# Loading the second half batch's q and k by head halves in 768-byte runs, in a rearranged opening

## The chip, the cores and the metric

The kernel runs on one core of a Trainium2 chip. The metric is device time in microseconds (us) of one execution. Engines are named as in the profile: PE is TensorE (its matmuls; PEld its weight loads), DVE is VectorE, ACT is ScalarE, POOL is GpSimd, SP is SyncE.

## The reference

Attention over q, k, v of shape (4 batches, 8 heads, 768 tokens, 64), each query seeing the first 8 keys and its last 96, with a slope times distance as bias; then a feed-forward layer on the 3072 x 512 result.

```python
scores = scale * np.matmul(q, k.transpose(0, 1, 3, 2))
keep = is_global | is_local            # pos < 8, or 0 <= rel < 96
scores = np.where(keep, scores - slopes[:, None, None] * dist, -1e9)
a = softmax(scores); attn = np.matmul(a, v)
x = attn.transpose(0, 2, 1, 3).reshape(B * S, H * D)
h = np.maximum(x @ w_in, 0.0)          # w_in 512 x 2048
out = (h * h @ w_out)                  # w_out 2048 x 512
```

## The kernel before, in words

The work goes by eight half batches of 384 tokens, three tiles of 128 tokens each: x0 and x1 are the halves of the first batch. For a tile, tokens lie on the partitions as loaded; PE transposes q and k so that the head dimension lies on the partitions (names `trp`), DVE or ACT copies the result from PSUM ("evacuates" it) to `q` and `k`. A query tile meets two key tiles: its own ("o") and the one before with the global keys in its first 32 columns ("b", kept in `kb`; its values in `vb`). Scores `sp` go through an exponential on ACT; attention `av`, its normalisation (a reciprocal `rec` and a product `tm` on DVE), a transpose (`trx`) and a copy give `xt`, the input of layer 1 (`hps`, L717), whose weights `w_in_sb` come in four quarters c0 to c3. Layer 2 is `yps`. Later half batches take other paths, which the change does not touch; large parts of their layers use sums of weights and of activations in place of products.

The opening, some 20 us, is the first batch's attention up to layer 1. It is written as jobs in the string `OPENING`: T0 and T1 transpose tiles 0 and 1 of q and k together; Q2 to Q5 and K2 to K5 one tile each; P are matmuls that put the bias into PSUM (tiles 0 to 2), S scores, A attention, X the transposes to `xt`, V the copies to `vb`. F and G are layer 1 of x0 (F of its first tile, G of the other two). So F0, G00 and G01 read c0; F1, G10 and G11 read c1; A50 and A51 are the attention of tile 5, which needs the values of tile 5 (v5).

Every operation on every engine, every load too, stands in one table, `ORDER`, written out as text ("p" PE, "a" ACT, "d" DVE, "s" SP, "l" a load on POOL, with numbers in the order of listing; behind the dot the PSUM banks). Each engine runs its operations strictly in that order. `LOADING` only gives the loads their numbers. Costs such as {"ACT": 0.51, "DVE": 0.36} stand beside operations and do nothing when the program runs.

The loads: SP and ACT issue four loads for tiles 0 and 1 (f32, then cast by `first_tiles`). All others are issued on POOL, which converts to f16 on the way: one tile of 128 tokens and 8 heads is 1024 runs of 256 bytes in memory (`rows`, L396), written as 128 bytes each; a quarter of `w_in` is 512 runs of 2 KB (L454). x1's q and k are staged in memory that `w_mix` uses later, so they are called w_mix in the profile. Loads on POOL take eight semaphores in turn, so that the ninth waits until the first has landed.

The copies are all one helper, L256 on ACT and L258 on DVE.

Of the kernel before, what the change touches and what calls it, by code (L numbers as in the profile page):

```python
# [9 lines left out]
FP16 = mybir.dt.float16  # L10
# [3 lines left out]
P = 128  # L14
# [5 lines left out]
OPENING = """T0 P1b T1 K3 P0o S0o S1b Q2 K2 P1o S1o P2o P2b A00 S2o A01 S2b Q5 Q3 A11 X01 Q4 V1 S3o A10  # L20
K4 X11 A20 X00 K5 X10 A21 S4o S4b S3b X21 X20 F1 G11 V2 S5o V3 S5b G10 F0 A40 V4 A30 G01 A41
# [4 lines left out]
LOADING = """v1 k3 k2 q2 v0 q3 q4 q5 k5 v2 k4 c1 v3 c0 v4 v5 c3 c2"""  # L26
# [30 lines left out]
a73 p29.6 d68 p18.5 d72 p28.4 a74 p26.3 l19 p36.1 d54 a69 p35.2 p30.7 a86 d70 p33.54 d85 a71 d91
p39.16 a67 p40.27 a77 d63 p37.3 a82 d75 l17 a78 d62 p41.5 a92 d79 d76 p38.0 d84 d80 p45.4 d83
l21 a97 p48.1 d96 a101 l20 a98 p44.2 a89 p47.5 d107 l23 p46.7 a112 p42.0 d111 a108 d110 a93
p43.2 d109 p53.1 a87 p52.5 d102 p50.4 p49.7 a113 l22 d120 d100 a90 d105 p59.6 l27 a116 d119 a103  # L60
d106 p55.3 p51.1 l29 d94 a122 a88 d128 p65.2 l28 a104 d95 a117 p64.4 a118 p58.5 a129 a136 d114
p60.0 d99 a137 l30 d146 d191 p54.3 l24 p62.6 d115 d205 l25 p57.1 a133 p56.4 d125 d121 p63.7
p67.6 a123 d134 d135 a130 d206 p61.1 p72.3 a126 d132 p69.4 d189 a124 p77.7 a131 d156 p70.0 a142
p82.1 d157 d165 a159 p71.5 a160 p74.4 d162 l34 a166 d201 a163 p83.6 d147 a161 l26 p73.0 a167
d522 d164 a138 p84.3 l31 d158 d148 a168 a169 p79.52 d186 l35 a139 d202 p89.04 p81.1 d127 a198
l33 d151 p85 a187 d170 a178 d523 p86 a174 d207 a199 d184 p78.06 a179 d149 l32 p80.57 p88.41 d180
p87 a195 l36 d200 a175 p76.2 d203 a185 l37 d155 p75.4 a196 d193 p91.0 l38 a188 d143 s194 d197
p66.1 a181 l39 d172 a171 p95.3 d152 a173 p90.5 d223 p100.4 d153 a209 s224 a176 d236 p92 d204
p103.2 d177 d208 p68.3 d237 s216 a244 a140 d210 p93.6 d240 a211 p94 a182 d150 s217 a144 d219
p96.1 p104 d225 p97 d183 a245 d221 p98.7 s220 d239 a218 p102.3 d238 p111 d214 d228 s226 l44 p106  # L70
d222 d243 l43 d213 p109.61 s229 d227 p110.73 d154 p99 l40@217 a255 d258 s215 d141 p101 a256
l42@217 d145 a251 d272 d190 p113 l45 a252 a234 p114.73 d254 l41@217 d192 p108.61 p105.0 a248 l46
d246 a261 p107 d253 d259 a262 l47 d257 s260 p115.62 a249 s235 d230 p116.74 l48 p118.3 a264 d250
p131.1 a265 d232 d263 p117.6 a268 d231 a292 p122.2 d266 a273 p121.7 d233 a269 d212 p125.1 a271
d280 s324 p124 d284 p127.4 a283 p126 d241 a278 d267 p123.6 d285 a293 p137.1 s325 d281 p119.5
a287 p132 a286 p129.7 a279 d294 p130 p140 d323 a301 p142 d270 p134.6 a290 d274 a307 p128.1 a291
p135 d288 p133.2 a308 p136 d298 p141.5 a310 d300 s242 a299 p143.1 s282 a297 d309 p139 d326 p138
d524 p112 d395 l50@325 a305 s275 d311 p120 a303 l56 d306 a312 s289 d295 a302 p146.36 l53 p147.54
d304 p145.71 a330 s296 d313 l51@325 a333 p144.2 a331 d318 l52 p148.3 a334 d319 a276 l49@325
p149.5 d321 a327 a322 d433 d332 a328 l54 p151.64 p150.07 d314 p152 d320 a338 l57 d329 p159.1  # L80
a339 l55 p157.0 d336 a337 p172.7 a341 d340 p153 a352 d370 a342 p160.3 a350 d315 p169.6 s371 d353
a344 p158.7 p162 d351 p161 p154.4 d316 a355 d397 p166.3 a347 p164.7 d356 p163 s398 p156 d317
d358 d359 a366 p171.1 d343 p165 s399 p167 a360 d362 p181.7 a363 d335 a361 p170 d345 p175 d367
p177 a357 p174.0 d375 p173.5 a378 d373 p178.3 s247 s277 d369 p176 a383 s354 p180 d368 a372
p155.0 d349 a379 p168.1 a376 d382 a384 d400 p179 p183 l58@399 a364 p182.7 d380 a348 p184 s374
a377 l65 d385 p185.3 a389 l62 a387 d381 s386 p188.41 a365 d388 p187.05 l59@399 p186.27 a405
p189.6 d401 a409 l63 a413 d402 p190.0 a406 d416 l73 a410 d403 p191 a407 l61 d396 a414 p193.42
d412 a417 p194.65 l60@399 d411 a418 p192.71 p195 a422 d415 a419 l64 d391 p200.4 d429 a420 p206.7
d437 a426 p198.0 d392 p219.1 s438 d393 a434 d408 a427 p207.6 p204.4 d394 a447 s346 d489 p210
d443 a462 p202.5 a451 d428 p199.1 a423 d404 p211 a441 p213 d435 p197.4 p217.2 a432 d456 p205.5  # L90
s436 p218.1 d424 a444 d452 p196 d480 s491 a445 d476 a461 d460 p203.6 p215.7 d442 p223 a458 p221
d425 a453 p208 d421 s492 p209 d481 p220 a448 d483 p222.1 a469 d477 p214 a446 d467 p227.6 s390
d431 s468 p212.0 d457 p201 d449 a464 d493 a463 p216.1 d454 p224 a484 l70 p225 d459 s455 p230
a439 d473 a471 l66 d465 p226 a496 p231.50 d470 a474 l69@492 s430 p236.13 d478 p233.42 a497 s490
p228.7 d472 a503 l72 d482 a498 p229.5 l67@492 a509 d479 d494 a504 p241.4 l71 p235 a510 d485 d475
a527 d505 p237.01 a495 l68@492 a466 p232.72 d499 p234 l74 a500 d525 d486 a450 p245.3 d506 l75
p240.7 d508 p247 a512 s507 d515 p246.5 a533 p239 d488 a532 d487 d516 a526 p255 a501 p250 d520
p259.0 d544 s521 p249.2 d531 p243.6 d536 p252 a535 p238.3 d529 a540 d517 a513 p253 a549 d502
p261.5 s576 a519 p256 d514 p257.6 p270 d545 p263 d546 p244 a551 s440 a553 d541 a565 p248.1 d511
a530 p268.6 p272 d561 p267 a534 p251.2 d560 p260.4 a566 s562 p262 d537 p269 d550 p258.6 a542  # L100
p266 s547 d548 p242.4 a563 d538 a568 p254.0 a552 s577 d518 p264 a528 p271 a578 d554 p274 d567
d543 p265.7 p273 d579 p275 a580 a555 d569 p279 d558 a564 p281.2 d556 a596 a570 p276.60 a559 d585
s557 d571 p277.54 p278.71 a586 p280 d600 a593 s539 a589 d601 p282.6 a604 d603 a587 p286 a594
d598 d602 a590 p284.75 a605 d588 p283.03 p285.14 a609 p289 d595 a616 a613 s599 d668 p291 s574
a606 d619 d581 a607 p288.7 d572 p290.1 d622 a610 s575 d582 p303.0 a620 d591 p306.3 a639 d612
s573 p294 d608 a618 a643 d611 p323.5 a614 d671 d626 p305.4 p307 d642 p310 a644 p292.6 d584 d621
p295 a623 p321.4 d583 a628 d647 p296 d664 p312 d615 p298 s665 a629 p301 d650 p287.1 d632 p308.3
a617 s627 p297.4 d636 s597 p322 d645 p313.2 a666 d592 p299.6 a651 d631 p314 a648 p293.0 d652
p311.4 d624 p300 p316 d649 p315 a635 s625 p318.0 a633 d669 p302.4 d672 p309 a634 d655 p320 a667
p304 d653 p326 a662 d637 p324.2 d658 s638 a679 p325.7 a663 d646 s659 d640 p317 a678 p319 p335.4  # L110
# [94 lines left out]
def kernel(  # L205
# [11 lines left out]
    nc = tc.nc  # L217
# [4 lines left out]
    NT = S // P  # L222
# [1384 lines left out]
```

## Time and profile before

| what | value |
|---|---|
| time, median of 3 runs | 200.62 us (200.59 to 200.8) |
| profiled execution, its own time | 200.43 us |
| its span | 198.7 us (1.73 us of its time lie around the span) |
| busy: PE, PEld, DVE, ACT, POOL | 191.6, 163.2, 176.3, 151.0, 66.9 us |
| granted PE clock | 1.0 in every slice |
| bytes by the POOL loads' queue | 13.11 MB in 74944 packets |

PE is the engine that matters if it never waits; so the table is read for where PE is not busy, which is the first 20 us and the last few. Windows of a few us, the timeline and the chain of waits then tell what it waits for there.

### The profile page before, as it was taken

To read this page: it belongs to the slowest core of one execution; us is meant where nothing else is said; L and a number is where in the kernel's file an instruction comes from. 1 tells how busy PE (TensorE), PEld (TensorE's weight loads), DVE (VectorE), ACT (ScalarE), POOL (GpSimd) and SP (SyncE) were. 2 spreads that over 40 slices of the span, in tenths; PEclk is the share of its full clock that TensorE was granted. 3 is DMA by queue.
4 is the path that set the end of the run, shared out by engine and by line. 5 is a ranking of instruction groups with operands and counts; after the bars stand their busy time and mean duration, and the time that the engine had idled before them with its cause. 6 is when DMAs were issued, how large, how long until landed. Compare 5 with 4: busy or idle time off the path is not lost.

```text
span 198.7 us, 5980 instructions
## 1 busy us (share of the span) xinstructions
PE 191.6 (96%) x2381; PEld 163.2 (82%) x2381; DVE 176.3 (89%) x450; ACT 151.0 (76%) x321; POOL 66.9 (34%) x82
## 2 busy tenths in 40 slices
PE   7798999999999999999999999999999999999993
PEld 3576899856888687788888998999889999999993
DVE  7589696899999999999989999899899996978971
ACT  6799797899555888976999679878897578769211
POOL 8996565187108701940194007800000000000000
PEclk9999999999999999999999999999999999999999
DMA  5999999999999998999899799996531221201214
GB/s 152 182 150 194 189 180 172 209 195 155 182 192 92 155 205 218 107 127 145 218 118 153 104 222 129 161 175 147 102 102 37 94 57 40 109 0 53 109 53 158
DMA packets 106987, 27.52 MB, mean 139 GB/s; under 512 B 97104, under 2 KB 104016, under 8 KB 106960
## 3 DMA queue, kind: packets, MB, share of 16 engines
q0 software_dynamic: 74944, 13.11, 90.1%
q1 hardware_dynamic: 30816, 13.45, 31.7%
q10 hardware_dynamic: 1200, 0.59, 1.1%
q8 instruction: 18, 0.29, 0.6%
q14 instruction: 9, 0.07, 0.1%
HBM read 27.26 MB, written 6.29 MB: 169 GB/s over the span
## 4 chain that ended last, share of the span: by engine, by line
PE 78%; DMA 7%; POOL 5%; DVE 5%; ACT 3%; issue 1%; POOLq 0%; DVEq 0%
PE yps L1064 32%; PE hps L841 19%; PE hps L717 14%; PE sp L610 4%; DMA xt<-tm 4%; DMA w_mix<-in_k_dram 4%; PE av L671 3%; PE yps L978 3%; POOL w_mix L396 2%; POOL v L396 1%; DVE hr L901 1%; ACT h L758 1%; PE av L1380 1%; PE trp L549 1%; DVE vb L258 1%
## 5 line engine op out<-in xcount | busy, mean ns | idle before, releaser
L623 ACT ACTIVATE ex<-sp 128x512 f16<-128x512 f32 x66 | 36.7, 632 | 3.6 <-PE sp L610 3.5
L1064 PEld LDWEIGHTS <-h 128*128 128x128 f16 x376 | 33.9, 98 | 4.0
L717 PE MATMUL hps<-xt,w_in_sb 128*128 128x128 f16 (+2 forms) x288 | 35.6, 273 | 0.3 <-ACT ex L1350 0.3
L256 ACT COPY kept<-hps 128x384 f32<-128x384 f32 x52 | 24.6, 490 | 12.4 <-PE hps L841 8.8
L901 DVE CUSTOM_DVE_ANT_0 hr<-hps,kept 128x384 f16<-128x384 f32 x58 | 30.3, 548 | 1.0 <-PE hps L841 0.6
L717 PEld LDWEIGHTS <-w_in_sb 128*128 128x128 f16 x288 | 23.5, 98 | 5.9 <-DMA w_in_sb<-in_moe_w_in_dram 0.5
L1064 PEld LDWEIGHTS <-mixed 128*128 128x128 f16 x272 | 25.2, 98 | 3.6 <-DVE mixed L1029 0.2
L396 POOL DMA_DIRECT2D sq<-in_q_dram x19 | 17.3, 910 | 31.0 <-DMA q<-sq 23.4
L256 ACT COPY y<-yps 128x256 f32<-128x256 f32 (+2 forms) x39 | 14.6, 385 | 15.8 <-PE yps L1064 15.8
L396 POOL DMA_DIRECT2D sk<-in_k_dram x19 | 17.1, 903 | 24.9 <-DMA q<-sq 22.4
L841 PEld LDWEIGHTS <-w_in_sb 128*128 128x128 f16 x288 | 24.4, 98 | 1.0
L841 PEld LDWEIGHTS <-in_mix 128*128 128x128 f16 x272 | 22.8, 98 | 1.1 <-issue 0.3
L841 PE MATMUL hps<-x_mix,in_mix 128*128 128x192 f16 x204 | 23.4, 246 | 0.0
L1064 PE MATMUL yps<-w_mix,h 128*128 128x256 f16 (+1 forms) x192 | 22.4, 264 | 0.0
L1064 PE MATMUL yps<-w_mix,mixed 128*128 128x256 f16 (+1 forms) x184 | 22.2, 268 | 0.0
L396 POOL DMA_DIRECT2D v<-in_v_dram x24 | 21.8, 922 | 1.2 <-DVE h L760 0.6
L1064 PE MATMUL yps<-w_out_sb,h 128*128 128x256 f16 (+1 forms) x184 | 21.9, 268 | 0.0
L924 ACT ACTIVATE h<-hr 128x768 f16<-128x768 f16 x25 | 20.9, 857 | 0.0
L647 DVE TENSOR_TENSOR phat<-ex,mask 128x1024 f16<-128x1024 f16 (+1 forms) x36 | 20.6, 590 | 0.1
L744 ACT ACTIVATE hr<-hps 128x384 f16<-128x384 f32 (+1 forms) x35 | 18.5, 546 | 2.8 <-PE hps L717 2.8
L841 PE MATMUL hps<-xt,w_in_sb 128*128 128x192 f16 x172 | 19.8, 246 | 0.0
L1126 DVE TENSOR_TENSOR y<-yps,y 128x256 f32<-128x256 f32 (+1 forms) x30 | 11.9, 408 | 3.5 <-PE yps L1064 2.9
(110 smaller groups left out, 354.1 us busy)
## 6 DMA issues: line engine op xcount, KB each, us to landing
out_dram<-y SPq DMA_DIRECT2D x23, 256.0 KB, 2.6
v<-in_v_dram POOLq DMA_DIRECT2D x24, 128.0 KB, 7.1
sq<-in_q_dram POOLq DMA_DIRECT2D x19, 128.0 KB, 6.4
sk<-in_k_dram POOLq DMA_DIRECT2D x19, 128.0 KB, 6.4
w_in_sb<-in_moe_w_in_dram POOLq DMA_DIRECT2D x4, 512.0 KB, 11.0
w_out_sb<-in_moe_w_out_dram POOLq DMA_DIRECT2D x4, 512.0 KB, 12.3
y<-in_q_dram SPq DMA_DIRECT2D x2, 256.0 KB, 4.4
y<-in_k_dram ACTq DMA_DIRECT2D x2, 256.0 KB, 5.1
```

What stands on the lines that cost most here:

```text
L256: nc.scalar.copy(out=out, in_=in_)
L396: dma = nc.gpsimd.dma_start(out=dst, in_=src[x.b, :, r0 + t * P:r0 + (t + 1) * P, :] .rearrange("h p d -> p h d"))
L610: nc.tensor.matmul(sp[h][:, i, :], lhsT=lhsT, rhs=x.q[rows, r % HT, a, :], start=True, stop=True)
L623: nc.scalar.activation(out=st["ex"][:, h], in_=sp[h], func=AF.Exp, scale=scale)
L647: eng(e).tensor_tensor(out=x.phat[a][:, :, t0:t0 + n], op=ALU.mult, in0=st["ex"][:, :, i0:i0 + 2 * n].rearrange("p e (t b) c -> p e t (b c ...
L717: nc.tensor.matmul(st["ps"][:, i * n:(i + 1) * n], lhsT=w_in_sb[:, kk, m * P:(m + 1) * P], rhs=x.xt[:, kk, c0:c1], start=kk == 0, stop=kk ...
L744: nc.scalar.activation(out=o, in_=i, func=AF.Relu)
L841: nc.tensor.matmul(st[name][:, i * HC:(i + 1) * HC], lhsT=left(i, kk), rhs=right(kk), start=fresh and i == kk == 0, stop=kk == KK - 1, ski ...
L901: eng(e)._custom_dve(dve_ops.TENSOR_ADD_SAT, out=hidden(which)[:, :, cols], in0=sums(name), in1=st[kept], s0=3.4e38, s1=0.0)
L924: nc.scalar.activation(out=h2, in_=hr, func=AF.Square)
L1064: nc.tensor.matmul(st[bank_name][:, 0:n], lhsT=a(m), rhs=b(m)[:, cols], start=fresh and m == 0, stop=m == HK - 1, skip_group_check=not fresh)
L1126: eng(e).tensor_tensor(out=y, in0=ps, in1=y, op=ALU.add)
```

## The change

x1's q and k are no longer loaded tile by tile (six loads of 1024 runs of 256 bytes), but by head halves (four loads, `heads`): partition p takes tokens 3p, 3p + 1 and 3p + 2 of four heads, 512 runs of 768 bytes. So a tile t of x1 is now every third token while it is staged. The loads land in a second staging area ("raw", heads outside, tokens inside); a new copy `by_tile` (128 x 768, f16 to f16, four in all, on DVE) puts a half into the old layout. `turn_heads` (jobs Q+0, Q+1, K+0, K+1) transposes two head pairs of all three tiles, six transposes, and one copy of 768 columns evacuates them; its input is read in steps (p a c t out of p a t c), so that the tokens come into their true order. Four such copies take the place of six of 512 contiguous columns. x1's q and k then lie head pair by head pair (`in_tokens`), which the score matmuls read by `keys` and `queries`. The number of transposes is the same. A few lines concern the tracking of buffers alone.

`ORDER` is a new table from end to end. From about 40 us on it is the old one with neighbours exchanged and PSUM banks renamed; in the opening it differs as follows.

The loads on POOL (names as above; w_mix from in_k and in_q are x1's k and q). Before:

```order
L396 DMA sq<-in_q_dram 128x8x64
L396 DMA w_mix<-in_k_dram 128x8x64
L396 DMA sk<-in_k_dram 128x8x64
L396 DMA w_mix<-in_q_dram 128x8x64
L396 DMA v<-in_v_dram 128x8x64 x2
L396 DMA w_mix<-in_q_dram 128x8x64
L396 DMA w_mix<-in_k_dram 128x8x64
L396 DMA v<-in_v_dram 128x8x64
L396 DMA w_mix<-in_q_dram 128x8x64
L396 DMA w_mix<-in_k_dram 128x8x64
L454 DMA w_in_sb<-in_moe_w_in_dram 128x4x512 x2
```

Now:

```order
L425 DMA w_mix<-in_k_dram 128x4x192 x2
L414 DMA sq<-in_q_dram 128x8x64
L414 DMA sk<-in_k_dram 128x8x64
L425 DMA w_mix<-in_q_dram 128x4x192 x2
L414 DMA v<-in_v_dram 128x8x64 x3
L491 DMA w_in_sb<-in_moe_w_in_dram 128x4x512 x2
L414 DMA v<-in_v_dram 128x8x64 x2
L491 DMA w_in_sb<-in_moe_w_in_dram 128x4x512 x2
L414 DMA sq<-in_q_dram 128x8x64
L414 DMA v<-in_v_dram 128x8x64
```

The same eleven tiles' bytes stand ahead of the first quarter of w_in, but x1's k comes first, then tile 2's q and k, x1's q, and only then the values v0, v1, v2. The first quarter was c1 and is c0 now. Behind v3 and v4 there were c3, a load of the next batch's k, v5, another k and c2; now both quarters c3 and c2 come ahead of v5, with one load (sq) between.

DVE behind the casts of the first tiles, before:

```order
L258 COPY k_142<-trp0_168 128x512 x2
L258 COPY k_142<-trp0_223 128x512
L258 COPY q_209<-trp0_245 128x512
L258 COPY kb_143<-k_142 128x16x32
L258 COPY q_280<-trp0_264 128x512
L258 COPY kb_143<-k_142 128x4x96
L258 COPY k_142<-trp0_240 128x512
L1392 RECIPROCAL rec_312<-av_297 128x2x2
L1394 TENSOR_TENSOR tm_314<-av_297,rec_312 128x256
L258 COPY vb_145<-v_144 128x520
```

Now:

```order
L258 COPY w_mix_109<-w_mix_109 128x3x256
L258 COPY q_203<-trp0_146 128x512
L258 COPY w_mix_109<-w_mix_109 128x3x256
L258 COPY kb_126<-k_125 128x16x32
L258 COPY kb_126<-k_125 128x4x96
L258 COPY k_125<-trp0_205 128x768
L258 COPY q_203<-trp0_267 128x512
L258 COPY k_125<-trp0_274 128x512
L258 COPY w_mix_109<-w_mix_109 128x3x256
L258 COPY kb_126<-k_125 128x4x96 x2
L258 COPY w_mix_109<-w_mix_109 128x3x256
L258 COPY q_336<-trp0_325 128x768
```

The four `by_tile` copies stand ahead of the first normalisation. Of the four evacuations behind T1, DVE had two and has one, ACT three. Of the four 768-column ones DVE has two and ACT two, where DVE had all six of the 512-column ones that they replace. Two of DVE's four slope constants went to ACT.

PE at the start of layer 1, before (the last scores of tile 5, then the first job of layer 1):

```order
L1330 LDWEIGHTS kb_143
L1330 MATMUL sp_519<-q_280,kb_143 128x128
L1330 LDWEIGHTS kb_143
L1330 MATMUL sp_520<-q_280,kb_143 128x128
L717 LDWEIGHTS w_in_sb_87
L717 MATMUL hps_533<-xt_388,w_in_sb_87 128x128
```

Now (the transposes of tile 2's normalised attention, then layer 1; line numbers are those of the changed kernel):

```order
L1475 LDWEIGHTS tm_465
L1475 MATMUL trx_491<-ident_82,tm_465 128x128
L1475 LDWEIGHTS tm_442
L1475 MATMUL trx_498<-ident_82,tm_442 128x128
L1475 LDWEIGHTS tm_442
L1475 MATMUL trx_498<-ident_82,tm_442 128x128
L754 LDWEIGHTS w_in_sb_87
L754 MATMUL hps_503<-xt_407,w_in_sb_87 128x128
```

Layer 1 began with F1 (c1) and all scores behind it; it begins with F0 (c0) now, and then come S4b and S5b, G00, F1 and A30. The first attention job that needs v5 stands behind four F and six G; it stood behind three F, seven G and three jobs of x1's layer 1.

The diff, cut to its core:

```diff
-LOADING = """v1 k3 k2 q2 v0 q3 q4 q5 k5 v2 k4 c1 v3 c0 v4 v5 c3 c2"""
+LOADING = """v1 k2 q2 v0 v2 k+0 q+0 k+1 q+1 c1 v3 c0 v4 v5 c3 c2"""
...
+        def heads(src, name, i, rank=None):
+            hs = slice(i * H // 2, (i + 1) * H // 2)
+            def emit(e):
+                staged(x, name)
+                return nc.gpsimd.dma_start(
+                    out=getattr(x, name + "_raw")[:, hs].rearrange("p h t d -> p h (t d)"),
+                    in_=src[x.b, hs, r0:r0 + HALF, :].rearrange("h (p t) d -> p h (t d)", t=HT))
+            load = plan.load(plan.FIRST_TOKENS, emit, before[name], rank)
+            def by_tile(e):
+                copy(e, staged(x, name)[:, :, hs],
+                     getattr(x, name + "_raw")[:, hs].rearrange("p h t d -> p t h d"))
+            return plan.add({"DVE": 0.3, "ACT": 0.75}, by_tile, [load])
...
+    def turn_heads(i, u):
+        st, both = {}, slice(2 * u, 2 * u + 2)
+        def emit(e):
+            st["ps"] = ps = bank([P, 2, HT, P], FP16, "trp0")
...
+            for a in range(2):
+                for t in range(HT):
+                    nc.tensor.transpose(
+                        out=ps[:, a, t, :],
+                        in_=(x1.sk if i else x1.sq)[:, t, 4 * u + 2 * a:4 * u + 2 * a + 2, :],
+                        identity=ident)
+        job = plan.pe(0.34, emit, [(x1.k_in if i else x1.q_in)[u], ident_op], 1)
+        op = plan.after(job, {"ACT": 0.69, "DVE": 0.50}, lambda e: copy(
+            e, in_tokens(turned_to(x1, i))[:, both].rearrange("p a (c t) -> p a c t", t=HT),
+            st["ps"].rearrange("p a t c -> p a c t")))
...
-                    lhsT = (bt.kb[rows, a, r - 2, :] if before and r > 1
-                            else bt.k[rows, r - before, a, :])
+                            else keys(bt, r - before)[rows, a, :])
```

More of the change, by code (lines that the diff above doesn't have):

```diff
@@ L14 @@
 P = 128
-OPENING = """T0 P1b T1 K3 P0o S0o S1b Q2 K2 P1o S1o P2o P2b A00 S2o A01 S2b Q5 Q3 A11 X01 Q4 V1 S3o A10
-K4 X11 A20 X00 K5 X10 A21 S4o S4b S3b X21 X20 F1 G11 V2 S5o V3 S5b G10 F0 A40 V4 A30 G01 A41
+OPENING = """T0 P1b T1 K+0 P0o S0o S1b Q2 K2 P1o S1o P2o P2b A00 S2o A01 S2b Q+0 K+1 A11 X01 Q+1 V1 S3o A10
+X11 A20 X00 X10 A21 S4o S4b S3b X21 X20 F1 G11 V2 S5o V3 S5b G10 F0 A40 V4 A30 G01 A41
 A31 G00 G30 X41 F3 X30 X31 A50 X40 F2 A51 E11 G31 G20 X50 G21 X51 E01 E10 D0 E00 D1"""
-LOADING = """v1 k3 k2 q2 v0 q3 q4 q5 k5 v2 k4 c1 v3 c0 v4 v5 c3 c2"""
+LOADING = """v1 k2 q2 v0 v2 k+0 q+0 k+1 q+1 c1 v3 c0 v4 v5 c3 c2"""
 PLACES = {2: (2.9, 8.0, 11.1, 12.4, 11.8, 11.3, 0, 0, 0, 0),
@@ L57 @@
[L57 to L62, printed above, removed]
@@ L123 @@
+a779 a780"""
 class Op:
@@ L345 @@
     batches = [Batch() for _ in range(B)]
+    for i, bt in enumerate(batches):
+        bt.b = i
     halves = [Half() for _ in range(NHB)]
@@ L375, in staged @@
             for i, n in enumerate(("sq", "sk")):
-                setattr(x, n, both[:, i].rearrange("p m d -> p (m d)")[:, 0:HT * H * D].rearrange(
-                    "p (t h d) -> p t h d", t=HT, h=H))
+                for part, n, form in ((i, n, "p (t h d) -> p t h d"),
+                                      (i + 2, n + "_raw", "p (h t d) -> p h t d")):
+                    setattr(x, n, both[:, part].rearrange("p m d -> p (m d)")[
+                        :, 0:HT * H * D].rearrange(form, t=HT, h=H))
         elif getattr(x, name, None) is None:
@@ L380, in staged, with in_tokens, keys, queries @@
         return getattr(x, name)
+    def in_tokens(block):
+        return block.rearrange("p t a c -> p (t a c)").rearrange("p (a n) -> p a n", a=NPAIR)
+    def keys(bt, r):
+        x = halves[2 * bt.b + r // HT]
+        if not x.spread:
+            return bt.k[:, r]
+        t = r % HT
+        return in_tokens(turned_to(x, 1))[:, :, t * P:(t + 1) * P]
+    def queries(x, t):
+        return in_tokens(x.q)[:, :, t * P:(t + 1) * P] if x.spread else x.q[:, t]
     def list_loads(x, first=None):
@@ L412, in list_loads @@
             x.k_in, x.q_in, x.v_in = [None] * HT, [None] * HT, [None] * HT
+            for i in range(2 * x.spread):
+                for src, name, key, ops in ((k, "sk", "k", x.k_in), (q, "sq", "q", x.q_in)):
+                    load_jobs[f"{key}+{i}"] = lambda src=src, name=name, ops=ops, i=i: (
+                        ops.__setitem__(i, heads(src, name, i)))
             for t in range(HT):
                 r = x.half * HT + t
-                if r > 1:
+                if r == 2:
                     for src, name, key, ops in ((k, "sk", "k", x.k_in), (q, "sq", "q", x.q_in)):
@@ L1275, in fix @@
         def fix(e):
-            copy(e, bt.kb[:, :, u - 1, GR:P], bt.k[:, u, :, GR:P])
-        kb_ops[u] = plan.add({"DVE": 0.36, "ACT": 0.45}, fix, [tile_ops[u][1]])
+            copy(e, bt.kb[:, :, u - 1, GR:P], keys(bt, u)[:, :, GR:P])
+        kb_ops[u] = plan.add({"DVE": 0.36, "ACT": 0.45}, fix, tile_ops[u][1::2])
     def turn_tile(r, i):
@@ L1295, in turn_tile @@
             fix_tile(r)
+    def turn_heads(i, u):
+        st, both = {}, slice(2 * u, 2 * u + 2)
+        def emit(e):
+            st["ps"] = ps = bank([P, 2, HT, P], FP16, "trp0")
+            warm(ps.rearrange("p a t c -> p (a t c)"))
+            for a in range(2):
[8 more added lines that the diff above has]
+            st["ps"].rearrange("p a t c -> p a c t")))
+        x1.turned.append(job)
+        for r in range(HT, NT):
+            tile_ops.setdefault(r, [None] * 4)[2 * u + i] = op
+        if len(x1.turned) == 4:
+            for r in range(HT, NT - 1):
+                fix_tile(r)
     def key_columns(r, before):
@@ L1312, in distances @@
         st["job", before] = plan.pe(H * (0.066 if r < 2 else 0.056), emit, slope_ops, 2)
+        slope_buf.used_by(st["job", before])
     def score_tile(r, before):
@@ L1328, in emit @@
                     lhsT = (bt.kb[rows, a, r - 2, :] if before and r > 1
-                            else bt.k[rows, r - before, a, :])
-                    nc.tensor.matmul(pair[h][:, a, :], lhsT=lhsT, rhs=halves[r // HT].q[rows, r % HT, a, :],
+                            else keys(bt, r - before)[rows, a, :])
+                    nc.tensor.matmul(pair[h][:, a, :], lhsT=lhsT,
+                                     rhs=queries(halves[r // HT], r % HT)[rows, a, :],
                                      start=not added, stop=not added or a == NPAIR - 1,
@@ L1343, in score_tile, with weighted @@
         st["bufs"] = [*st.get("bufs", []), ph_buf]
-        st["ph", before] = phat_p.tile([P, 2, NPAIR, P], FP16, name="ph0", tag="ph0")
+        def weighted():
+            if ("ph", before) not in st:
+                st["ph", before] = phat_p.tile([P, 2, NPAIR, P], FP16, name="ph0", tag="ph0")
+            return st["ph", before]
         for h in range(2):
@@ L1349, in ex @@
                                                    bufs=4)
-                nc.scalar.activation(out=st["ph" if added else "ex", before][:, h],
+                nc.scalar.activation(out=(weighted() if added else st["ex", before])[:, h],
                                      in_=st["sp", before][h], func=AF.Exp, scale=scale)
@@ L1358, in weigh @@
             a_ = slice(a0, a0 + 2)
-            eng(e).tensor_tensor(out=st["ph", before][:, :, a_], in0=st["ex", before][:, :, a_],
+            eng(e).tensor_tensor(out=weighted()[:, :, a_], in0=st["ex", before][:, :, a_],
                                     in1=m[:, :, a_, c0:c0 + P], op=ALU.mult)
@@ L1486 @@
                 for h in range(H)]
+    slope_buf = Buffer("ex", 4)
+    slope_buf.used_by(*slope_ops[1:])
     for op in [*slope_ops, *mask_ops, *first]:
```

137 lines of the change are left out of this document (73 added, 64 removed).

## The prediction

> **What bounds the kernel now.** I read the page first, then windows, then the chain of waits over the first 40 us, then the timeline engine by engine. The page gives span, PE's busy tenths in 40 slices, and the engines' shares of the chain that ended last:
>
> ```profile
> span 198.7 us, 5980 instructions
> PE   7798999999999999999999999999999999999993
> ...
> PE 78%; DMA 7%; POOL 5%; DVE 5%; ACT 3%; issue 1%; POOLq 0%; DVEq 0%
> ```
>
> PE is short of work only in the first four slices and the last. Windows (start to end; length; busy us of PE, PEld, DVE, ACT, POOL) say the same:
>
> ```profile
> 15.00:20.00 5.00, 4.09 (x85) 3.17 (x80) 4.79 (x17) 4.66 (x13) 3.20 (x4) 1.00 1.43 195
> 25.00:30.00 5.00, 5.00 (x80) 4.59 (x77) 4.83 (x17) 4.61 (x11) 3.44 (x5) 1.00 1.84 182
> 40.00:60.00 20.00, 19.99 (x227) 14.96 (x226) 19.48 (x49) 14.97 (x33) 8.18 (x10) 1.00 1.84 180
> ```
>
> From 20 us on PE does not wait. The matmuls are the same ones in both kernels, so the question is one number: how much earlier or later PE gets into that dense stretch, counted by work done. The chain of waits (start, length, what) shows who admits it there:
>
> ```profile
> 10.59 6.97 DMA w_mix<-in_k_dram
> ...
> 17.60 0.62 PE trp L1287 x8
> ...
> 20.09 4.54 PE hps L717 x48
> ...
> 25.36 0.89 PE hps L717 x16
> ...
> 33.27 0.24 PE av L1380 x8
> 33.51 0.87 PE hps L717 x8
> ```
>
> The last of x1's k, issued at 10.59, lands at 17.56; behind it come transposes and `xt`, and layer 1 begins at 20.09. An F job takes 0.89 us, a G job 0.87. The weights arrive no earlier: in the timeline PEld's wait names them.
>
> ```profile
> 20.07 1.99 PEld L717 LDWEIGHTS <-w_in_sb 128*128 128x128 f16 x27 [0.47 <-DMA w_in_sb<-in_moe_w_in_dram]
> ...
> 28.72 4.55 PE L717 MATMUL hps<-xt,w_in_sb 128*128 128x128 f16 x48
> ```
>
> So two things end together at 20.07 us: the first batch's attention and the first quarter of w_in. Both hang on the loads.
>
> **Part 1, the loads.** POOL's rows (its own time per issue), then the packets done from 8 to 12 us and from 16 to 20 us:
>
> ```profile
> 1.37 1.04 POOL L396 DMA_DIRECT2D sq<-in_q_dram  x1
> ...
> 11.46 1.55 POOL L454 DMA_DIRECT2D w_in_sb<-in_moe_w_in_dram  x2
> ...
> 20.31 0.75 POOL L454 DMA_DIRECT2D w_in_sb<-in_moe_w_in_dram  x1 [1.57 <-DMA w_in_sb<-in_moe_w_in_dram]
> ...
> 28.97 1.48 POOL L461 DMA_DIRECT2D w_out_sb<-in_moe_w_out_dram  x2 [0.25 <-DMA v<-in_v_dram]
> ```
>
> ```profile
> DMA packets 4806, 0.61 MB, mean 152 GB/s; under 512 B 4806, under 2 KB 4806, under 8 KB 4806
> ...
> DMA packets 861, 0.81 MB, mean 202 GB/s; under 512 B 81, under 2 KB 861, under 8 KB 861
> ```
>
> POOL issues the first quarter at 11.46 and it lands at 20.07, so the DMA engines are behind, not POOL, and cheaper issues save nothing by themselves. A 128-byte write costs one engine 4 us x 16 / 4806 = 13.3 ns; a 1 KB write (64 - 81 x 0.0133) / 780 = 80.7 ns. On the line between, one of 384 bytes is 32.6 ns. Six tile loads were 6 x 1024 x 13.3 / 16 = 5.11 us; four head loads are 4 x 512 x 32.6 / 16 = 4.17. Saved: 0.94, I take 0.9. Bounds: 0 if long runs move no more bytes per us than short ones, and 4 x (1.28 - 0.97) = 1.24 us if they move as many as the 2 KB runs.
>
> The eleven tiles ahead of the first quarter are the same bytes, so it lands at 20.07 - 0.9 = 19.2. It is c0 now. After F0, S4b, S5b and G00 comes F1, which needs c1. A quarter is 0.52 MB at 202 GB/s, 2.6 us; the second one landed by 20.07 + 0.89 + 2 x 0.87 = 22.7 (PE used it then without a wait). In the new order that makes c1 21.8. Before, the work that precedes F1 now (F, G, all scores) was done at 20.07 + 0.89 + 0.87 = 21.83. So at F1 the gain by loads is about **0.0 us**.
>
> The second gate is v5. Before, the issue at 28.97 waits for the load eight before it, which is v5; issue follows landing by 0.24 (20.31 against 20.07), so v5 landed at 28.7. Now c2 comes ahead of it and the next batch's load is one either way: 28.7 - 0.9 + 2.6 = 30.4. The work that precedes A50 now (four F, six G) was done at 28.72 + 0.89 + 0.89 = 30.5. Gain **0.1 us**. Before, the first attention that reads v5 ran at 33.27, so the old order had 4 us of slack there; this one has none. c3 and c2 come earlier than before and wait for nobody.
>
> **Part 2, the engines up to F0.** A job of scores takes 0.34 us, from 9.07 to the next job on PE:
>
> ```profile
> 9.07 0.40 PE L1330 MATMUL sp<-q,k 64*128 64x128 f16 x8 [0.91 <-ACT q L256]
> ...
> 9.41 0.40 PE L1287 MATMUL trp<-ident,w_mix 128*128 128x128 f16 x4
> ```
>
> F1 follows F0 by 0.89 + 2 x 0.34 + 0.87 = 2.4 us, so F0 may start at 21.8 - 2.4 = 19.4 without loss. Do the engines bring it by then? The rows of DVE, and behind them one on how far x1's loads lay behind their issue:
>
> ```profile
> 8.21 1.29 DVE L258 COPY k<-trp 128x512 f16<-128x512 f16 x2 [1.55 <-PE trp L1244]
> ...
> 11.55 0.41 DVE L258 COPY q<-trp 128x512 f16<-128x512 f16 x1
> 11.88 0.47 DVE L258 COPY kb<-k 128x384 f16<-128x384 f16 x1
> ...
> 13.14 0.86 DVE L258 COPY vb<-v 128x520 f16<-128x520 f16 x2
> 13.93 0.23 DVE L258 COPY kb<-k 128x384 f16<-128x384 f16 x1
> ...
> 16.15 0.65 DVE L258 COPY kb<-k 128x384 f16<-128x384 f16 x1
> ...
> 17.26 0.17 DVE L1392 RECIPROCAL rec<-av 128x4 f32<-128x4 f32 x1
> 17.46 0.42 DVE L1394 TENSOR_TENSOR tm<-av,rec 128x256 f16<-128x256 f32 x1
> 17.81 0.17 DVE L1392 RECIPROCAL rec<-av 128x4 f32<-128x4 f32 x1
> ```
>
> ```profile
> DMA to landing us min/median/max: 6.3/6.4/7.0
> ```
>
> From start to start: a contiguous evacuation of 512 is 0.33 (11.55 to 11.88); T1's stepped one 0.64 (1.29 / 2); a normalisation 0.55 (17.26 to 17.81); the `vb` pair 0.79 (13.14 to 13.93). The new 768-column evacuation reads in steps like T1's: 0.11 + 768 / 512 x 0.53 = 0.9 (the bounds: 0.46 as if contiguous, 0.96 by plain scaling). `by_tile` is f16 from SBUF to SBUF like `kb`, whose 384 columns take 0.23 alone and 0.47 or 0.65 at other times, for a cause the rows don't name; twice the columns are then about 0.3 to 0.72, I take 0.42 between starts. DVE's new list from k+0's landing (1.4 + 6.4, a little more for its larger share of bytes: 8.1 us) to the last normalisation ahead of F0: 4 x 0.42 + 0.64 + four `kb` 1.4 + 2 x 0.9 + 2 x 0.33 + 0.79 + 6 x 0.55 + one `xt` 0.2 = 10.5, so 18.6 us. Two X jobs (0.2) and the steps between engines (0.1) behind it: F0 at **18.9 us**, 0.5 inside the limit.
>
> One rule speaks against this part. The Trainium skill (SBUF — State Buffer, Who interferes with whom) says that a DVE copy in a two-port mode and GpSimd share a pair of ports as an exclusive lock, and that the later one blocks fully. By its letter each `by_tile` under an issue of POOL could wait out up to 0.9 us of it, which by 4 x 0.9 us would make the time some 203. The `kb` rows all stand under POOL's issues and show 0 to 0.42 us more, so the trace bears out a part of it at most.
>
> ACT takes over three evacuations and two slopes:
>
> ```profile
> 4.49 0.92 ACT L337 ACTIVATE mask<-dmask 128x384 f16<-128x384 f32 x2
> ...
> 5.31 0.49 ACT L331 ACTIVATE slope_id<-ident 128x128 f16<-128x128 f16 x2
> ...
> 7.10 0.62 ACT L256 CAST sk<-y 128x512 f16<-128x512 f32 x1 [1.30 <-DMA y<-in_k_dram]
> 7.62 0.93 ACT L337 ACTIVATE mask<-dmask 128x384 f16<-128x384 f32 x2
> ...
> 12.24 3.06 ACT L1350 ACTIVATE ph<-sp 128x512 f16<-128x512 f32 x6
> ...
> 15.15 0.64 ACT L1350 ACTIVATE ex<-sp 128x512 f16<-128x512 f32 x1
> ```
>
> Between starts a mask is 0.41, a cast 0.52, an exponential 2.91 / 6 = 0.485; a slope I put at 0.2, an evacuation at 0.48, one of 768 at 0.64 (both by the exponential's row and its columns). 8 x 0.41 + 6 x 0.2 + 0.52 + 3 x 0.48 + 2 x 0.64 + 10 x 0.485 = 12.6 from about 3.4 us: tile 2's last exponential ends at 16.0, where it ended at 15.2. The old list waited 1.30 us for the second half of k; the new one does slopes and masks there. A20 and A21 need that exponential and their `vb` (16.2 on DVE's list), so ACT is level with DVE and does not decide.
>
> PE's own start, S0o, stood at 9.07 and comes at about 9.3 (k's evacuation waits behind four masks until 8.5, q's behind `by_tile`). It is a part of the chains above, not a further term.
>
> Behind F0 DVE has the weights' products (`ph`), a `vb` pair and a `kb` to do before A30 and A40; 0.2 us of waiting there I take from 0 to 0.4. The six freed 512-column evacuations and tile 2's earlier q and k are in the lists already. From 40 us on I cost the table at nothing, between -0.2 and 0.2: PE had no idle time there, and the order is the old one with neighbours exchanged.
>
> **The sum.** At F1 0.0, at A50 0.1 earlier, stalls at A30 and A40 0.2 later: 0.1 us later in all, 200.5 on the profiled execution's 200.43. That execution ran 0.19 us under the median, so I forecast 200.62 + 0.1, about **200.7 us**: no measurable change, where 0.2% (0.4 us) is about what a measurement can tell.
>
> **Rivals.**
> *The loads speed up as 2 KB runs do (faster).* 1.24 us saved, somewhat more on the slowest engine, say 1.4: c1 at 21.3, where the engines' F0 at 18.9 also puts F1; v5 at 29.9. Both gates give 0.5 to 0.6, so 200.1. For it: both chains of Part 2 leave that room. Against it: the line through the two packet prices.
> *The long runs bring nothing (slower).* c1 at 22.7, 0.9 late; v5 at 31.3, 0.8 late: 201.5. It decides as soon as the saving is under 0.5 us. For it: the byte rate rises only by a third between 128 bytes and 1 KB, and 384 is nearer to the short end.
> *DVE's copies wait for POOL's issues (slower).* With `by_tile` and `kb` at their long ends (0.72 and 0.57 between starts) the list is 1.2 + 0.9 longer, F0 at 21.0, 1.6 behind its limit: 202.2; half of that gives 200.62 + 0.6 = 201.2. It decides from 19.8 on for F0. For it: DVE is busy 4.79 of 5 us before 20 already, and POOL issues throughout. The rule of the SBUF page above is this mechanism at its worst.
> *The change does nothing* is not among them: the loads and the copies are in the built program.
>
> **How the numbers follow.** Both gates within 0.4 us of the old ones: 0.42, 200.7, own range 200.2 to 201.0. Faster by loads: 0.27, 200.1 (199.5 to 200.2). Slower by loads that don't gain: 0.13, 201.5. Slower by DVE's waits: 0.18, 201.2 (to 202.2; the full wait of 0.9 us at each copy, some 203, is 0.03 of it). So faster 0.27, same 0.42, slower 0.31. The range leaves out the far ends on both sides: 199.9 to 201.7.
>
> **What would show it.** In the changed kernel's profile: the head loads' packets at 384 bytes, and the wait of PEld for w_in ending near 19.2 and near 21.8; F0 at or after 19.2; v5's attention near 30.4, with a wait on DMA v; `by_tile` near 0.45 us and the 768-column copies near 0.9 on DVE; tile 2's last exponential near 16.0. The forecast is wrong if w_in's first wait ends behind 19.8 or well before 18.9, if F0 waits for DVE's `tm` beyond 19.8, or if PE has new idle time behind 36 us.

## The result, and the profile after

The changed kernel took 202.47 us (median of 15 runs, 201.1 to 203.48), the kernel before, beside it, 200.06 us (15 runs, 199.77 to 201.01). The ratio is 1.0114, 95% interval 1.0091 to 1.0137: 2.4 us slower, where 200.7 us was forecast with a range up to 201.7 (the forecast stood 0.1 us above the 200.62 that the kernel before had taken; beside the changed kernel it took 200.06). The profiled execution of the changed kernel took 201.1 us; it is the fastest of the 15, which span 2.4 us, so it shows only a part of the loss (0.67 us against the 200.43 of the profile before).

From the page of the changed kernel, the span, PE's busy tenths and the shares of the chain that ended last:

```profile
span 199.3 us, 5975 instructions
PE   7898999999999999999999999999999999999993
...
PE 72%; DVE 15%; ACT 6%; DMA 3%; issue 2%; POOL 1%; DVEq 0%; POOLq 0%
```

The tenths look as before, but the chain runs through DVE for 15% of the span instead of 5%. Windows of 5 us say where PE lost time. First before, then after (busy us of PE, PEld, DVE, ACT, POOL; clock; share; GB/s):

```profile
45.00:50.00 5.00, 5.00 (x69) 3.77 (x69) 4.72 (x11) 4.41 (x9) 3.58 (x5) 1.00 2.42 154
50.00:55.00 5.00, 5.00 (x66) 4.39 (x63) 4.92 (x11) 2.79 (x7) 0.80 (x1) 1.00 2.13 185
```

```profile
45.00:50.00 5.00, 4.68 (x50) 3.02 (x47) 4.27 (x10) 4.04 (x8) 4.95 (x6) 1.00 2.25 154
50.00:55.00 5.00, 4.86 (x52) 4.15 (x49) 4.97 (x13) 3.46 (x7) 0.89 (x1) 1.00 2.19 184
```

PE has 0.46 us of new idle time between 45 and 55 us, which is one of the signs that the prediction named for being wrong. What PE and PEld wait for there, in the timeline after:

```profile
49.76 0.19 PE L708 MATMUL av<-v,phat 128*128 128x65 f16 x1 [0.32 <-DMA v<-in_v_dram]
...
53.77 0.77 PEld L1101 LDWEIGHTS <-mixed 128*128 128x128 f16 x8 [0.42 <-DVE mixed L1066]
```

The first wait is for a load: the values of the second batch. The second follows from the same loads. DVE's copies of these values wait for them too, and all that stands behind them in DVE's list moves by that:

```profile
48.73 0.73 DVE L258 COPY vb<-v 128x520 f16<-128x520 f16 x2 [0.70 <-DMA v<-in_v_dram]
```

In the profile of experiment 1 below, which has two of the values early, these copies start at 47.90, and the `mixed` behind them at 52.22, where it is 53.02 here.

The POOL timelines show why the values are late, and that the last quarter of w_out, which layer 2 needs, is issued late with them (in this fastest run PE has no wait for it). Before:

```profile
32.18 0.74 POOL L461 DMA_DIRECT2D w_out_sb<-in_moe_w_out_dram  x1 [1.73 <-DMA w_in_sb<-in_moe_w_in_dram]
33.48 1.90 POOL L396 DMA_DIRECT2D v<-in_v_dram  x2 [0.56 <-DVE h L760]
39.42 0.88 POOL L396 DMA_DIRECT2D sq<-in_q_dram  x1 [4.04 <-PE trp L549]
40.28 0.88 POOL L396 DMA_DIRECT2D v<-in_v_dram  x1
...
45.75 0.88 POOL L396 DMA_DIRECT2D sk<-in_k_dram  x1 [1.65 <-DMA w_out_sb<-in_moe_w_out_dram]
```

After:

```profile
29.94 0.74 POOL L498 DMA_DIRECT2D w_out_sb<-in_moe_w_out_dram  x1 [0.37 <-DMA v<-in_v_dram]
39.50 0.89 POOL L414 DMA_DIRECT2D sq<-in_q_dram  x1 [8.81 <-PE trp L586]
40.38 0.76 POOL L498 DMA_DIRECT2D w_out_sb<-in_moe_w_out_dram  x1
41.12 2.65 POOL L414 DMA_DIRECT2D v<-in_v_dram  x3
```

The load `sq` of the fourth half batch may only go when x2's transposes have read the old `sq`, at 39.4 us in both. The new table has it ahead of the fourth w_out load and of all three values; the old one had it behind that w_out load and two values. POOL works its list in order, so they were issued at 40.38 and 41.12 instead of 32.18 and 33.48. By then the DMA engines had run short of work. The window 40 to 42 us, before and then after:

```profile
40.00:42.00 2.00, 2.00 (x12) 0.91 (x10) 2.00 (x9) 2.00 (x8) 2.00 (x3) 1.00 1.23 201
```

```profile
40.00:42.00 2.00, 2.00 (x25) 1.04 (x22) 2.00 (x10) 1.97 (x6) 2.00 (x4) 1.00 0.75 59
```

There 59 GB/s are moved instead of 201. And the order before had little room there: by the last row of the list before, the w_out load eight issues earlier landed about 45.5 us (issue follows landing by 0.24), and PE uses it at 45.83:

```profile
45.83 1.04 PE L978 MATMUL yps<-w_out_sb,h 128*128 128x512 f16 x4
```

### The profile page after: what moved, and what is told of

Same layout as the page of the kernel before. It is cut to its first block, busy times and chain, and to the rows that moved or that the text cites. A ratio compares the mean times of both kernels' runs of the same rounds, so it can differ in the third digit from the quotient of the medians.

```text
span 199.3 us, 5975 instructions
## 1 busy us (share of the span) xinstructions
PE 192.5 (97%) x2381; PEld 163.8 (82%) x2381; DVE 179.8 (90%) x454; ACT 150.6 (76%) x319; POOL 64.5 (32%) x80
## 4 chain that ended last, share of the span: by engine, by line
PE 72%; DVE 15%; ACT 6%; DMA 3%; issue 2%; POOL 1%; DVEq 0%; POOLq 0%
PE yps L1101 31%; PE hps L878 21%; PE hps L754 9%; PE av L708 3%; DMA v<-in_v_dram 3%; PE sp L647 3%; DVE hr L783 2%; ACT mask L337 2%; DVE mixed L1066 1%; DVE tm L1460 1%; DVE vb L258 1%; PE yps L1015 1%; DVE in_mix L822 1%; PE av L1446 1%; PE sp L1391 1%
## 5 line engine op out<-in xcount | busy, mean ns | idle before, releaser
L754 PE MATMUL hps<-xt,w_in_sb 128*128 128x384 f16 (+2 forms) x288 | 36.0, 272 | 0.0
L938 DVE CUSTOM_DVE_ANT_0 hr<-hps,kept 128x384 f16<-128x384 f32 x58 | 30.4, 549 | 1.0 <-PE hps L878 0.6
L256 ACT COPY y<-yps 128x256 f32<-128x256 f32 (+2 forms) x40 | 15.1, 390 | 15.6 <-PE yps L1101 13.7
L878 PE MATMUL hps<-xt,w_in_sb 128*128 128x192 f16 x172 | 19.8, 246 | 0.0
L795 ACT ACTIVATE h<-hr 128x512 f16<-128x512 f16 (+1 forms) x23 | 16.3, 730 | 3.3 <-DVE hr L783 2.3
L781 ACT ACTIVATE hr<-hps 128x384 f16<-128x384 f32 (+1 forms) x29 | 15.0, 540 | 2.5 <-PE hps L754 2.4
```

The lines of the kernel that those rows point to most:

```text
L256: nc.scalar.copy(out=out, in_=in_)
L754: nc.tensor.matmul(st["ps"][:, i * n:(i + 1) * n], lhsT=w_in_sb[:, kk, m * P:(m + 1) * P], rhs=x.xt[:, kk, c0:c1], start=kk == 0, stop=kk ...
L781: nc.scalar.activation(out=o, in_=i, func=AF.Relu)
L795: nc.scalar.activation(out=h2, in_=hr, func=AF.Square)
L878: nc.tensor.matmul(st[name][:, i * HC:(i + 1) * HC], lhsT=left(i, kk), rhs=right(kk), start=fresh and i == kk == 0, stop=kk == KK - 1, ski ...
L938: eng(e)._custom_dve(dve_ops.TENSOR_ADD_SAT, out=hidden(which)[:, :, cols], in0=sums(name), in1=st[kept], s0=3.4e38, s1=0.0)
```

## The experiments

In the diffs a line is the order of loads on POOL. `l27` and `l28` are the third and fourth w_out load of the changed kernel, `l22` to `l24` the second batch's values, `l32` the blocked `sq`, `l42` the first `sq` of the fifth half batch. In the kernel before the same loads are `l28`, `l30`, `l24` to `l26`, `l34` and `l44`. A wait that an edit adds is written out in brackets. Each time is a median; the ratio is to the kernel before, run beside it.

**1. Both put back ahead.**

```diff
-l27 l32 l28 l22 l23 l24
+l27 l28 l22 l23 l32 l24
```

> The changed kernel with one thing of its table put back: on POOL the last quarter of w_out and the first two values of the second batch stand ahead of the sq of the fourth half batch again, as before the change. That sq waits for x2's transposes, 8.81 us in the changed kernel's profile, and what stands behind it waits with it. Theory A (the queue behind the blocked sq is the loss): about 200.3 us (199.9 to 200.9), spread of the runs under 1.3 us, PE idle between 40 and 60 us back from 0.47 to under 0.1 us. Theory B (the opening's gates without slack, v5 and the quarters c2 and c3, are the loss, different from run to run): 202.3 us as the changed kernel, same spread. Theory C (the rest of the table, later on): 202 us or more.

Measured: 200.94 us (200.29 to 201.58), ratio 1.0033 (1.0015 to 1.0052). Against the changed kernel's 202.47 that is 1.5 of the 2.4 us. PE was busy all of 40 to 60 us. So theory A holds for the greater part, though the time lies just above its range, and 0.33% stays. B and C, as the main cause, fall.

**2. Only the last quarter of w_out ahead.**

```diff
-l27 l32 l28 l22 l23 l24
+l27 l28 l32 l22 l23 l24
```

> Only the last quarter of w_out is put ahead of the blocked sq; the three values stay behind it. Theory A, if the late w_out (weight sums 4 us late on DVE) carries it: most of the gain, 200.3 to 200.9 us; if the late values carry it: the values are issued only 0.76 us earlier, 201.3 to 202.3 us. Theories B and C: 202.3 us.

Measured: 201.07 us (200.82 to 201.45), ratio 1.0035 (1.0012 to 1.0058): 1.4 us less, a little above the range for it, and its 12 runs lie within 0.63 us. By the medians the late w_out carries most of the loss. DVE's weight sums, which the expectation named, do not: they start at 44.14 here, and at 44.00 in the profile after. The late values still show in this profile, as a wait of PE for `mixed` of 0.40 us at 53.68.

**3. Only two values ahead.**

```diff
-l27 l32 l28 l22 l23 l24
+l27 l22 l23 l32 l28 l24
```

> Only the first two values are put ahead of the blocked sq; the last quarter of w_out and the third value stay behind it. Theory A, if the late values carry it: 200.3 to 201 us, the third value is issued 1.8 us earlier than in the changed kernel; if the late w_out carries it: 201.5 to 202.3 us. Theories B and C: 202.3 us.

Measured: 201.84 us (200.96 to 202.58), ratio 1.0082 (1.0053 to 1.0112): 0.6 us less. Here PE's timeline shows what the fastest run of the changed kernel did not, the wait of layer 2 for w_out:

```profile
47.38 1.02 PE L1015 MATMUL yps<-w_out_sb,h 128*128 128x512 f16 x4 [0.56 <-DMA w_out_sb<-in_moe_w_out_dram]
```

The gains of 2 and 3 (1.4 and 0.6) add up to more than that of 1 (1.5). That would fit two waits that lie partly beside each other; no run shows it directly.

**4. The mirror: the kernel before with both moved behind.**

```diff
-l28 l30 l24 l25 l34 l26
+l28 l34 l30 l24 l25 l26
```

> The mirror: the kernel before, whole, but with its last quarter of w_out and two values moved behind the blocked sq, the order of the changed kernel. Theory A: 201.2 to 202.5 us, with a spread over 1.3 us and new idle time of PE between 40 and 60 us. Theories B and C: 200.1 to 200.4 us, no change.

Measured: 202.07 us (201.53 to 204.41), ratio 1.0109 (1.0066 to 1.0152). The old loads, the old opening and the old table, with the blocked `sq` moved ahead of three loads, give the changed kernel's time. PE was busy 18.43 of the 20 us from 40 to 60.

**5. The mirror with w_out alone** (run last, of twelve).

```diff
-l28 l30 l24 l25 l34 l26
+l28 l24 l25 l34 l30 l26
```

> The kernel before with its last quarter of w_out alone moved behind the blocked sq, the first two values left ahead of it. In the changed kernel, putting that quarter alone ahead took 1.4 us off, putting two values alone ahead 0.6 us. If the late w_out carries the loss here too: 201.0 to 201.7 us, with DVE's weight sums late and PE idle between 45 and 56 us. If the late values carry it: 200.0 to 200.4 us.

Measured: 202.24 us (201.74 to 204.08), ratio 1.0117 (1.0066 to 1.0168), more than either theory gave. The profile (201.84 us, 1.55 above the kernel before) has one new wait of PE between 40 and 60 us, and it is longer than that loss:

```profile
47.80 1.02 PE L978 MATMUL yps<-w_out_sb,h 128*128 128x512 f16 x4 [2.16 <-DMA w_out_sb<-in_moe_w_out_dram]
```

with its cause on POOL:

```profile
39.53 0.88 POOL L396 DMA_DIRECT2D sq<-in_q_dram  x1 [5.61 <-PE trp L549]
40.40 0.76 POOL L461 DMA_DIRECT2D w_out_sb<-in_moe_w_out_dram  x1
```

Issued at 40.40, landed at 47.8, needed at 45.6. DVE's weight sums, which the expectation named, stood where they stood before (from 39.66 us on); PE's own read of w_out is what is late.

**6. and 7. What remains: do the next loads meet a transfer?** In the profile of the first experiment PE's row at 61.7 us, behind the whole opening, stands where the kernel before has it. Before, and then experiment 1:

```profile
61.68 1.05 PE L1064 MATMUL yps<-w_out_sb,h 128*128 128x256 f16 x8
```

```profile
61.70 1.05 PE L1101 MATMUL yps<-w_out_sb,h 128*128 128x256 f16 x8
```

The same row starts at 62.50 in the profile after, and at 62.41 and 62.31 in those of experiments 2 and 3, which each have one of the two still late.

In experiment 1 PE then loses 0.30 us at 67.9, waiting for the transfer of x2's activations to `xt`, and 0.33 at 82.1, waiting for a `tm` of DVE. The fifth half batch's loads went out at 59.02 there, at 60.44 before.

```diff
-l42
+l42 (waits for x2's last tm)
```

> On top of the first experiment's order (last quarter of w_out and two values ahead of the blocked sq): the fifth half batch's first load, sq, now waits for x2's last normalisation (tm), which in the first experiment's profile began at 60.11 while the loads went out from 59.02; in the kernel before they went out at 60.44, behind it. Theory D (what remains, 0.9 us, is that the earlier loads meet the last transfer of x2's activations to xt, which then landed 0.5 us late for PE at 67.4): 200.1 to 200.5 us, and no wait of PE on xt near 67. Theory E (what remains lies in the opening's gates or in DVE's list up to 60 us): 200.9 us as in the first experiment.

Measured: 200.66 us (199.72 to 201.42), ratio 1.0016 (0.9989 to 1.0042). Inconclusive: the interval holds both theories.

```diff
-l42
+l42 (waits until x2's last xt transfer has landed)
```

> As the one before, but the sq waits until the last xt transfer has landed, so that the loads can't meet it at all. Theory D: PE's wait near 67 gone, 200.0 to 200.5 us unless the loads, some 3 us later, hold up the fifth half batch's transposes at 70 us (then above 201 us). Theory E: 200.9 us or more.

Measured: 204.7 us (203.65 to 206.09), ratio 1.0230 (1.0183 to 1.0277). The loads went out at 64.34, 5.3 us later, and were too late for DVE's copy of their values, so for PE:

```profile
78.88 0.20 PE L708 MATMUL av<-v,phat 128*128 128x65 f16 x1 [2.66 <-DVE phat L684]
```

The same edit in the kernel before (two loads moved behind the transfer, and the wait):

> The kernel before with the same wait: the fifth half batch's two sq stand behind x2's last xt transfer and wait until it has landed. Theory D: the runs of the kernel before at 200.8 to 201.8 us (7 of 24) go away, median 199.7 to 200.0 us. Theory E, or the loads coming too late: 200.1 us or more, with the same spread.

Measured: 204.37 us, ratio 1.0213 (1.0176 to 1.0251), PE idle 3.30 us at the same place. There the loads went out 4.2 us later than before (64.60 against 60.44). Neither kernel has that much room, so this wait tells nothing about the collision.

**8. All three values ahead.**

```diff
-l27 l28 l22 l23 l32 l24
+l27 l28 l22 l23 l24 l32
```

> On top of the first experiment's order the third value of the second batch too stands ahead of the blocked sq, earlier than in either kernel. Theory A in full (late values still cost something in the first experiment and in the kernel before, where DVE waited 0.24 us for that value at 47.4): 0.1 to 0.4 us under the first experiment, 200.5 to 200.8 us. If the first experiment has taken out all of that: 200.9 us.

Measured: 200.55 us (199.82 to 201.4), ratio 1.0019 (0.9996 to 1.0042): 0.4 us under experiment 1 by the medians, inside theory A's range, but not to be told from experiment 1 by the intervals.

**9. to 11. The change alone.** With all of the loads put right in both kernels (all values ahead, `l42` or `l44` behind `tm`), they differ in the change and its opening alone.

> The changed kernel with everything of the loads put right together: last quarter of w_out and all three values of the second batch ahead of the blocked sq, and the fifth half batch's sq behind x2's last tm. Theories A and D together (the two took 0.4 and 0.3 us off the first experiment's 200.94 us, one at a time): 200.0 to 200.4 us, level with the kernel before. Theory E (the opening or DVE's list costs something by itself): 200.5 us or more.

> The kernel before with the same two steps (third value too ahead of its blocked sq, fifth half batch's sq behind x2's last tm), so that it differs from the ninth experiment only in the change itself, with the rearranged opening. Theories A and D: 199.7 to 199.9 us with fewer runs above 200.7 us. If the kernel before has nothing to gain there: 199.95 to 200.1 us. The difference between the two is the change's own worth: 0.0 by the prediction's sum (+0.1 us), over 0.5 us by theory E.

> The kernel before with the third value ahead of its blocked sq and nothing else. Theory A: DVE's wait of 0.24 us for that value at 47.4 goes; 199.7 to 199.9 us. If that wait lies beside other work: 199.95 us, no change.

Measured, beside the same runs of the kernel before: the changed kernel 200.65 us (199.9 to 200.95), ratio 1.0014 (0.9995 to 1.0033); the kernel before so arranged 200.64 us (199.82 to 201.06), ratio 1.0009 (0.9990 to 1.0028); with the third value alone 200.25 us, ratio 1.0005 (0.9983 to 1.0027). The first two are level. But both lie above theory A's and D's ranges, and experiment 9 lies in theory E's (200.5 or more); that experiment 10 is as high speaks against E's 0.5 us for the change itself, and the intervals (0.4 us either way on each) do not exclude it. Experiment 11 left DVE's wait where it was, 0.22 us at 47.35: it was never for the third value. In the profile before, the third value landed at 49.3 (issued at 40.28, 9.0 us to landing), and DVE's copy started at 47.64, as the second landed. No version beat the kernel before.

What stays open is the rest, and whether it is one thing. Experiment 1, with these loads in the order before, lies 0.3 to 1.0 us (0.15 to 0.52%) above the kernel before; experiments 9 and 10 are level. In the profiles the rest is a wait of 0.2 to 0.5 us, behind 50 us, at a place that changes from run to run, and some (experiment 9's, 200.07 us) have next to none. The new opening has one wait of its own: in five of its eight profiles (experiments 1, 2, 3, 7, 8) PE waits for the first batch's values, 0.20 to 0.68 us at a time and ahead of F0. v0 to v2 stand behind all of the opening's q and k now, and the prediction gave their landing no term. F0 starts between 18.95 and 19.21 us in all eight, latest where that wait is longest (experiment 8).

## Why the prediction was wrong, point by point

*PE's dense stretch, and the question how much earlier it is entered: borne out, within the noise.* PE was busy 4.97, 5.00, 5.00 and 4.95 of 5 us in the four windows from 20 to 40 us. PE's row of 61.7 us above starts at 61.63 in experiment 9 and at 61.74 in experiment 10, and by their medians the change itself is worth 0.0 us, where the sum had +0.1; by their intervals that is good to about 0.5 us.

*Part 1, the loads: the price right, two landings forecast too late.* The packets of 384 bytes dominate here after:

```profile
6.00:8.00 2.00, 1.63 (x27) 1.35 (x24) 1.80 (x4) 2.00 (x7) 2.00 (x3) 1.00 1.61 189
10.00:11.00 1.00, 1.00 (x27) 0.90 (x24) 0.89 (x2) 1.00 (x3) 1.00 (x2) 1.00 1.60 191
```

190 GB/s are 384 x 16 / 190 = 32.3 ns a packet; the line between the two old prices gave 32.6. But c1 and v5 landed earlier than worked out:

```profile
21.08 0.88 POOL L414 DMA_DIRECT2D sq<-in_q_dram  x1 [1.46 <-DMA w_in_sb<-in_moe_w_in_dram]
```

This issue waits for c1, eight before it: about 20.8 us, forecast 21.8. In the same way the w_out row at 29.94 above puts v5 at 29.7, forecast 30.4. The old second quarter "by 22.7" was a bound, used as if it were a landing. It cost nothing, since engines, not loads, set the start.

*Part 2, the engines: F0 right, in part by two misses that cancel.* F0 was forecast at 18.9 us; PEld's and PE's rows:

```profile
18.77 0.29 PEld L1475 LDWEIGHTS <-tm 128*128 128x128 f16 x4 [0.23 <-DVE tm L1460]
...
19.07 1.05 PE L754 MATMUL hps<-xt,w_in_sb 128*128 128x128 f16 x16
```

It comes behind DVE's `tm`, without a wait for w_in. DVE's new copies, with 768 columns:

```profile
7.56 0.41 DVE L258 COPY w_mix<-w_mix 128x768 f16<-128x768 f16 x1
...
8.61 0.84 DVE L258 COPY w_mix<-w_mix 128x768 f16<-128x768 f16 x1
...
9.95 0.94 DVE L258 COPY k<-trp 128x768 f16<-128x768 f16 x1
...
11.86 0.84 DVE L258 COPY w_mix<-w_mix 128x768 f16<-128x768 f16 x1
...
13.26 0.41 DVE L258 COPY w_mix<-w_mix 128x768 f16<-128x768 f16 x1
13.59 0.93 DVE L258 COPY q<-trp 128x768 f16<-128x768 f16 x1
```

The stepped evacuations took 0.94 and 0.93 (forecast 0.9 between starts; the second, with the next row right behind it, 0.85). `by_tile` took 0.41 twice and 0.84 twice. Between starts, as the forecast counted, that is 0.33 to 0.76, the upper end just over its bound of 0.72; the four come to 2.29 us where the sum had 4 x 0.42 = 1.68. Against that DVE's list began at 7.56 instead of 8.1. So the last normalisation ahead of F0 ended at 18.71, forecast 18.6. Two of the four copies took 0.43 us longer than the others. The rule of the Trainium skill that was weighed there (SBUF — State Buffer, Who interferes with whom) would by its letter have given up to 0.9 us for each copy. Whether POOL's issues are the cause of the 0.43 us is not shown, since POOL was issuing under one of the short copies too (6.47 to 9.18 us). Tile 2's last exponential ended at 16.1, forecast 16.0.

*"Behind F0", 0.2 us of stalls: inside its bounds, at their low end.* PE lost 0.03 us from 20 to 25 us and 0.05 from 35 to 40. Its one wait at an attention in the profile after (0.26 us for DVE's `vb`, at 16.37) lies ahead of F0. A50 started at 30.56, where the sum gives 30.4 and 0.2 of stalls, and found v5.

*"From 40 us on I cost the table at nothing, between -0.2 and 0.2": this step failed.* Experiments 1, 4 and 5 put 1.5 to 2.0 us there, of the 2.4; where the rest lies, here or in the opening, stays open as said. Its ground was that PE had no idle time there and that the order was the old one with neighbours exchanged. The first says that PE didn't wait in the old order, not how late a load may come. The second was not so on POOL: the blocked `sq` had moved ahead of three loads, the last quarter of w_out and two values (with the third value, four stand behind it now). The change was walked through POOL's queue only up to v5. The rows to price it stood in the profile before: the `sq` issued at 39.42 behind a wait for `trp`, the fourth w_out landing at 45.5, PE at 45.83. An estimate from them, made with the result known: issued behind that `sq`, at 40.4, with the 6.3 us that the prediction's row has as the shortest landing, and without or with 2.6 us more for its own bytes, the quarter comes between 46.7 and 49.3 us, 0.9 to 3.5 us late. Experiments 4 and 5 measured 2.0 and 1.95 us more time.

*The rivals.* None of them has the queue behind the blocked `sq`. The third, DVE's copies waiting for POOL (201.2 to 202.2 us, chance 0.18), lies nearest to the time, and its cause is refuted: F0 came at 19.07, before its point of decision (19.8).

## What to carry to other kernels

When a written-out order changes, read each in-order queue to its end, DMA queues first: for every load that waits for an engine, list what stands behind it, when that lands and when it is first used. A consumer that never waits in the profile says nothing about its slack; the slack is read from the row in which a later issue waits for the landing, against the row of first use (here 45.5 against 45.83 us).

## What was not expected of the hardware

PE's granted clock fell after a stall of 2.66 us, but not after one of 2.16 us. Windows of experiment 7 (the loads behind the landed xt), behind the stall that ended at 78.88 (clock before the share of the DMA engines):

```profile
78.00:80.00 2.00, 1.12 (x17) 0.95 (x18) 1.93 (x6) 0.00 (x0) 0.00 (x0) 1.00 1.22 259
80.00:82.00 2.00, 2.00 (x10) 1.04 (x8) 2.00 (x7) 0.90 (x2) 0.43 (x1) 0.53 0.92 245
82.00:84.00 2.00, 2.00 (x11) 1.32 (x10) 1.93 (x7) 1.32 (x4) 2.00 (x3) 0.61 0.51 66
```

and experiment 5 (w_out alone late), behind the stall that ended at 47.80:

```profile
48.00:50.00 2.00, 2.00 (x13) 1.10 (x12) 1.14 (x3) 1.20 (x2) 1.50 (x2) 1.00 2.43 155
```

At 0.53 and 0.61 for 2 us each, PE does by estimate 1.7 us less work; with the stall that is 4.4 us, where experiment 7 lay 3.8 us above experiment 1 and 4.7 above the kernel before. So a stall can cost much more than its length. Whether the length alone decides it is not shown, with one profile of each: the clock's mean over the run stayed at 1.0 in two of experiment 7's six runs, and in experiment 5 it fell to 0.992 in two of six, which took 203.92 and 204.08 us where the other four took 201.74 to 202.64. The Trainium skill (TensorE: Matmul & The Clock Gate, Part 1) has the clock halve after at least one idle window of about 3.4 us that runs free. The half clock agrees, but here a stall of 2.66 us was enough.

The last quarter of w_out took 13.3 us to land when it was issued at 32.18 (45.5, kernel before) and 7.4 us when it was issued at 40.40 (47.8, experiment 5): issued 8.2 us later, it landed 2.3 us later.
